# Native float32 transforms in place of split ones, and four weight tiles converted at other places

## The chip, the cores and the metric

The kernel runs on one core of a Trainium2 chip. The time is that of one execution on the device, in microseconds (us). The engines work side by side, each through its own list of instructions in order: TensorE (PE) multiplies matrices, VectorE (DVE) and ScalarE (ACT) work elementwise, GpSimd (POOL) does elementwise work and issues DMAs, SyncE (SP) issues DMAs.

## The reference

Three layers follow one another. Attention has 4 batches, 8 heads, 512 local and 32 global tokens and a head width of 64; the middle layer is a gated feed-forward with a convolution of width 3 over the tokens; the last mixes tokens and features by a Fourier transform, then has a layernorm and an MLP.

```python
# x: attention output, [4, 544, 512]
h = np.maximum(x @ w_in, 0.0)                       # w_in [512, 1024]
conv_out[:, s] = sum(conv_w[k] * h[:, s + k - 1] for k in range(3))
x = (h / (1.0 + np.exp(-conv_out))) @ w_out         # w_out [1024, 512]
mixed = np.real(np.fft.fft(np.fft.fft(x, axis=1), axis=2))
u = x + mixed
un = (u - mean(u)) / np.sqrt(var(u) + 1e-06)
out = u + np.maximum(un @ w_ch1, 0.0) @ w_ch2       # 512 -> 2048 -> 512
```

All weights come as float64. A tile of weights is made from their raw 32-bit halves on the chip.

## The kernel before, in words

**Splitting.** The products of the middle layer and the MLP keep both factors as two rounded parts (`fp32r`), high and low, and `mm3` (L145) issues three matmuls for each product: low by high, high by low, high by high. In attention the matmuls take plain float32 (`mm` alone), as the scores of `s_mm` (L284): two row blocks and two heads, 224 columns each, a head on 64 of the 128 rows. L339 and L340 are float32 transposes.

**Weight tiles.** The MLP has 32 of them, 0 to 15 of `ch1` and 16 to 31 of `ch2`, each 512 KB raw. To make one, `fetch` has SP load the raw tile; `from_f64` takes ACT L164, POOL L165, ACT L167 and DVE L171 and L172; `put` writes the high part by ACT (L200) and the low part by DVE (L201). Tiles KEEP1 to 31 are converted during the attention steps (`keep_load`, `keep_make`, `keep_store`; the first of them at step KEEP0, then one each two steps) and put into device memory (`kept`). Later POOL loads them from there (`fetch_c`, L731). The others are fetched and converted (`make_c`) from the last MoE units on, and in the first NCONV = 5 steps of the MLP.

**The stages.** Attention and most of the MoE run interleaved, in an order written out by hand. Then comes the MoE tail: the loop over units u (64 units, 16 for each batch; each has `m_g1` into one PSUM bank `g1`, relu h at L482, the convolution on ACT and DVE at L492 to L494, tanh at L500, the gate g at L511 to L513, and `m_g2`). With it run four blocks a unit of the first transform. The MLP has 128 steps v, 16 for each chunk c of 272 tokens: `c_g1` (banks `g1` and `pv` in turn), relu and split into `hdt` (L798, L799), `c_g2` into the banks a0 to a3 with a tile `w_v`. The three other transforms run in its first five steps. From the MoE tail on, a scheduler orders the instructions by priority and by the places in SBUF that they need.

**The transform.** `fft(b)` is a generator of 13 pieces for one batch. It folds the tokens (L653, L656, L657 on DVE), splits the folded tile `ff` into `fh` and `fl` (ACT L654, L658; DVE L655, L659), multiplies with the constants c2, s2 and the single row co (six blocks of 256 or 258 columns), takes each block from PSUM as a high part by ACT (L672, L679) and a low part by DVE (L673, L680) into `ab`, and multiplies these with c1 and s1 (five blocks of 274 columns, DVE evacuates: L693, L696, L703, L706, L714, L715). The blocks go to the banks `s` and `t` in turn. In the trace c2 and c1 are both called `c`, s2 and s1 both `s`. Constants are split as well, so a block takes nine matmuls for three products.

**Places.** Some places in SBUF have names, v16 to v31; raw tiles, weight tiles and the tiles of the transform take them one after another. A tile that takes a place waits until all readers of the one before are done.

## Time and profile before

| | |
|---|---|
| median of three runs | 836.88 us (836.75, 836.88, 844.13) |
| profiled execution | 841.99 us, span 840.2 us |
| mean granted clock of PE | 0.968 |
| PE busy | 789.2 us (94% of the span) |
| DVE busy | 463.1 us (55%) |
| ACT busy | 372.2 us (44%) |
| POOL busy | 213.5 us (25%) |

The profiled execution is one of its own, so its time stands beside the median of the others. The clock is a share of full speed, 2.4 GHz: 1.00 is the upper level, 0.50 the lower (1.2 GHz). A busy share is a mean over stages that differ, so the sections below go by stretches. A matmul's own duration is that of one in flight; several overlap, and their price is the time from start to start.

### The profile page before, as it was taken

The numbers are of one execution on the slowest core, as the hardware profiler recorded it, in microseconds if no ns is written. First come the engines' busy times: TensorE is split into PE (matmuls) and PEld (weight loads), VectorE is DVE, ScalarE is ACT, GpSimd is POOL, SyncE is SP. The second block draws the span as 40 slices with busy tenths as digits, with TensorE's granted clock in tenths as the row PEclk, the third lists the DMA queues.
The fourth block names the chain that finished last, engine by engine and source line by source line (L and its number), as shares of the span: only waits on it lengthen the run. The fifth ranks groups of instructions, "written<-read, shape, count | busy, mean of one in ns | idle before, by whom it ended". The sixth has DMA issues, their size and how long they took to land.

```text
span 840.2 us, 16148 instructions
## 1 busy us (share of the span) xinstructions
PE 789.2 (94%) x6436; PEld 741.4 (88%) x6436; DVE 463.1 (55%) x1202; ACT 372.2 (44%) x947; POOL 213.5 (25%) x274
## 2 busy tenths in 40 slices
PE   5769999999999989987798999999999999999997
PEld 3458889899889879986697999999999999999997
DVE  5898987778777785699797531222222122222212
ACT  5677776666666765666652132121211212121110
POOL 4554443222222230122241252040402204030100
PEclk9789999999999998998988999999999999999999
DMA  7743341354136420664301700000000000000000
GB/s 248 265 151 112 127 160 57 113 176 156 40 109 207 145 76 2 176 183 125 126 1 50 253 27 1 2 27 1 28 1 28 2 1 27 1 28 1 27 2 27
DMA packets 32299, 69.06 MB, mean 82 GB/s; under 512 B 2728, under 2 KB 19496, under 8 KB 32224
## 3 DMA queue, kind: packets, MB, share of 16 engines
q1 hardware_dynamic: 29664, 59.08, 20.8%
q0 software_dynamic: 2560, 8.94, 3.6%
q8 instruction: 51, 0.84, 0.4%
q14 instruction: 24, 0.20, 0.1%
HBM read 57.65 MB, written 10.75 MB: 81 GB/s over the span
## 4 chain that ended last, share of the span: by engine, by line
PE 62%; DVE 14%; DMA 11%; ACT 9%; issue 2%; POOL 1%; SPq 0%; DVEq 0%; ACTq 0%; POOLq 0%
PE ps_a L143 28%; PE ps_g L143 16%; PE ps_pv L143 11%; DMA raw_r<-in_ch_dram 6%; PE ps_s L143 4%; ACT pb L318 3%; PE ps_t L143 2%; DVE y L493 2%; DVE pb L306 2%; DMA raw_w<-in_ch_dram 1%; DVE y L494 1%; DVE mag L172 1%; DMA co<-in_co_dram 1%; ACT mag L164 1%; DVE mag L171 1%
## 5 line engine op out<-in xcount | busy, mean ns | idle before, releaser
L143 PE MATMUL ps_a<-hdt,w_v 128*128 128x272 f32 x1536 | 215.3, 289 | 0.2 <-DVE w_v L201 0.2
L143 PEld LDWEIGHTS ps_a<-hdt,w_v 128*128 128x128 f32 x1536 | 202.2, 190 | 0.5 <-DVE w_v L201 0.5
L143 PE MATMUL ps_g<-xh,w_w 128*128 128x256 f32 (+1 forms) x512 | 116.0, 305 | 3.6 <-ACT h L482 3.5
L143 PE MATMUL ps_a<-g,w_w 128*128 128x254 f32 (+1 forms) x768 | 113.4, 296 | 5.0 <-ACT g L512 4.9
L329 POOL TENSOR_SCALAR pb<-pb,sm 128x224 f32<-128x224 f32 x128 | 83.2, 666 | 134.9 <-DVE sm L324 105.7
L143 PE MATMUL ps_g<-chl,w_w 128*128 128x272 f32 x768 | 108.1, 288 | 0.9 <-DVE chl L763 0.9
L143 PEld LDWEIGHTS ps_a<-g,w_w 128*128 128x128 f32 x768 | 103.4, 193 | 6.3 <-ACT g L512 5.4
L143 PE MATMUL ps_pv<-chl,w_w 128*128 128x272 f32 x768 | 107.0, 288 | 0.0
L143 PEld LDWEIGHTS ps_g<-chl,w_w 128*128 128x128 f32 x768 | 100.7, 188 | 1.3 <-DVE chl L763 1.1
L143 PEld LDWEIGHTS ps_pv<-chl,w_w 128*128 128x128 f32 x768 | 100.5, 188 | 0.0
L143 PEld LDWEIGHTS ps_g<-xh,w_w 128*128 128x128 f32 x512 | 87.2, 194 | 13.6 <-issue 7.9
L799 DVE SCALAR_TENSOR_TENSOR hdt<-ps_pv,hdt 128x272 fp32r<-128x272 f32 x64 | 28.2, 440 | 125.5 <-ACT hdt L798 125.5
L799 DVE SCALAR_TENSOR_TENSOR hdt<-ps_g,hdt 128x272 fp32r<-128x272 f32 x64 | 28.0, 438 | 113.3 <-ACT hdt L798 113.3
L798 ACT ACTIVATE hdt<-ps_pv 128x272 fp32r<-128x272 f32 x64 | 25.3, 396 | 139.5 <-PE ps_pv L143 134.2
L798 ACT ACTIVATE hdt<-ps_g 128x272 fp32r<-128x272 f32 x64 | 25.4, 397 | 135.6 <-PE ps_g L143 130.1
L143 PE MATMUL ps_g<-xl,w_w 128*128 128x256 f32 (+1 forms) x256 | 75.6, 295 | 0.0
L820 POOL TENSOR_TENSOR misc<-misc,u 128x272 f32<-128x272 f32 x28 | 19.3, 719 | 213.0 <-DVE misc L819 213.0
L318 ACT ACTIVATE pb<-pb,sm 128x224 f32<-128x224 f32 x128 | 60.4, 475 | 12.8 <-DVE sm L306 12.7
L165 POOL TENSOR_SCALAR mag<-mag 128x512 f32<-128x512 f32 x36 | 28.8, 801 | 93.3 <-ACT mag L164 92.7
L143 PE MATMUL ps_s<-qk 64*128 64x224 f32 (+1 forms) x144 | 38.0, 427 | 13.8 <-DMA qk<-in_qk_dram 6.7
L143 PEld LDWEIGHTS ps_g<-xl,w_w 128*128 128x128 f32 x256 | 49.8, 195 | 0.0
L493 DVE SCALAR_TENSOR_TENSOR y<-h,convw,y 128x254 f32<-128x254 f32 (+1 forms) x64 | 35.2, 550 | 16.2 <-ACT y L492 16.0
(206 smaller groups left out, 1269.4 us busy)
## 6 DMA issues: line engine op xcount, KB each, us to landing
v<-in_v_dram SPq DMA_DIRECT2D x16, 640.0 KB, 4.6
raw_w<-in_ch_dram SPq DMA_DIRECT2D x16, 512.0 KB, 3.7
qk<-in_qk_dram SPq DMA_DIRECT2D x16, 464.0 KB, 6.0
raw_r<-in_ch_dram SPq DMA_DIRECT2D x12, 512.0 KB, 6.3
kept<-w_o SPq DMA_DIRECT2D x12, 512.0 KB, 5.3
w_v<-kept POOLq DMA_DIRECT2D x12, 512.0 KB, 4.7
qk<-in_qk_dram SPq DMA_DIRECT2D x16, 304.0 KB, 6.0
out_dram<-misc SPq DMA_DIRECT2D x32, 136.0 KB, 1.7
```

Source lines behind the costliest of these rows:

```text
L143: return pe.matmul(o, a, b, start=start, stop=stop)
L164: act.activation(mag, f32(head), AF.Abs, scale=65536.0)
L165: (clamp or dve).tensor_scalar(mag, mag, TOP, 2.0, op0=ALU.min, op1=ALU.max)
L171: dve.scalar_tensor_tensor(val, val, 3, tail, op0=ALU.logical_shift_left, op1=ALU.bitwise_or)
L172: dve.scalar_tensor_tensor(val, head, -(2**31), val, op0=ALU.bitwise_and, op1=ALU.bitwise_or)
L306: anchor[i] = dve.tensor_tensor_reduce(out=pbs(i)[h][:, a, 0:224], in0=sb[h][:, a], in1=mask[:, 2 * where(i)[1] + a], scale=-0.125, scalar ...
L318: act.activation(p, p, AF.Exp, bias=sm[:, k:k + 1], scale=-1.0, accum_out=sm[:, 4 + k:5 + k])
L329: gp.tensor_scalar(p, p, sm[:, k:k + 1], 1.0, op0=ALU.mult, op1=ALU.mult)
L493: dve.scalar_tensor_tensor(y, hb[:, cc - 1:cc - 1 + n], convw2[:, m, 0:1], y, op0=ALU.mult, op1=ALU.add)
L798: act.activation(hd[:, 0], o, AF.Relu)
L799: dve.scalar_tensor_tensor(hd[:, 1], o, 0.0, f32(hd[:, 0]), op0=ALU.max, op1=ALU.subtract)
L820: (dve if c == 7 else gp).tensor_add(o, o, u_t[b][:, e, HS * half:HS * half + HS])
```

## The change

The transforms take float32 as it is. The splits of the folded tile and of the blocks are gone (`ff`, `fh`, `fl` become one tile `fi` written by DVE; `ab` holds one copy made by ACT), the constants are not split and half as large, and each product is one native matmul. The constants are loaded by SP and no longer by POOL. Tile 19 is one more that is converted in attention (KEEP0, KEEP1 = 8, 19). Tiles 16 to 18 are fetched at the start of the MoE tail into places v29 to v31, which the transform no longer needs, and converted in units 56 to 58, ahead of tiles 0 to 7. In the first MLP steps tiles 8 to 15 alone are converted. The places of the transform's tiles are dealt anew: c2 and s2 share v20, c1 has v21, s1 v24, `fi` v22 and v23 in turn, `ab` v25 and v27 in turn.

```diff
--- before.py
+++ after.py
@@ -31,7 +31,7 @@
 SOLO = 8
 LAG_G2 = 3
 NCONV = 5
-KEEP0, KEEP1 = 10, 20
+KEEP0, KEEP1 = 8, 19
 NPB, NHB = 3, 3
 MT = [(0, 92), (92, 92), (184, 90)]
 
@@ -52,17 +52,6 @@
     t2 = (DM - p) % DM
     t2[0] = DM // 2
     return np.concatenate([p, 128 + p, t2, DM // 2 + 128 - p])
-
-
-def _round12(x):
-    m, e = np.frexp(np.asarray(x, np.float64))
-    return np.ldexp(np.round(m * 4096.0) / 4096.0, e)
-
-
-def _split(x):
-    hi = _round12(x)
-    lo = _round12(x - hi)
-    return np.stack([hi, lo], axis=-2).astype(np.float32)
 
 
 def _constants():
@@ -105,10 +94,10 @@
     s1[:, 272] = 0.0
 
     def tok(x):
-        return _split(x.reshape(3, 92, NF).transpose(1, 0, 2))
+        return x.reshape(3, 92, NF).transpose(1, 0, 2).astype(np.float32)
 
     def feat(x):
-        return _split(x.reshape(2, 128, -1).transpose(1, 0, 2))
+        return x.reshape(2, 128, -1).transpose(1, 0, 2).astype(np.float32)
 
     return {
         "ident": np.eye(128, dtype=np.float32),
@@ -630,12 +619,13 @@
     frp = right.enter_context(tc.tile_pool(name="frp", bufs=1, side="right"))
     u0 = frp.tile([128, 4, 546], F32, name="u0")
     fp = right.enter_context(tc.tile_pool(name="fp", bufs=1, side="right"))
-    c2 = fp.tile([128, 2, 2, 258], F32R, tag="v20", name="c2")
-    s2 = fp.tile([128, 2, 2, 256], F32R, tag="v21", name="s2")
-    co = fp.tile([1, 258], F32R, name="co")
-    c1 = fp.tile([128, 2048], F32R, tag="v25", name="c1")
-    s1 = fp.tile([128, 2048], F32R, tag="v27", name="s1")
-    c1, s1 = [t[0:92, 0:6 * NF].rearrange("p (t s k) -> p t s k", t=3, s=2) for t in (c1, s1)]
+    c2s2 = fp.tile([128, 1028], F32, tag="v20", name="c2s2")
+    c2 = c2s2[:, 0:516].rearrange("p (c k) -> p c k", c=2)
+    s2 = c2s2[:, 516:1028].rearrange("p (c k) -> p c k", c=2)
+    co = fp.tile([1, 258], F32, name="co")
+    c1 = fp.tile([128, 1024], F32, tag="v21", name="c1")
+    s1 = fp.tile([128, 1024], F32, tag="v24", name="s1")
+    c1, s1 = [t[0:92, 0:3 * NF].rearrange("p (t k) -> p t k", t=3) for t in (c1, s1)]
     u_t = {}
 
     turn = itertools.cycle("st")
@@ -645,39 +635,29 @@
 
     def fft(b):
         eo = eo_t[b]
-        ff = fp.tile([128, 1024], F32, tag="v24", name="ff")
-        fe = fd = ff[:, 0:2 * NF].rearrange("p (c n) -> p c n", c=2)
-        fh = fp.tile([128, 4, NF], F32R, tag="v22", name="fh")
-        fl = fp.tile([128, 4, NF], F32R, tag="v23", name="fl")
+        fi = fp.tile([128, 4, NF], F32, tag=f"v{22 + b % 2}", name="fi")
         rev = slice(S, S - NF, -1)
-        dve.tensor_add(fe, eo[:, 0:2, 0:NF], eo[:, 0:2, rev])
-        act.copy(fh[:, 0:2], fe)
-        dve.tensor_sub(fl[:, 0:2], fe, f32(fh[:, 0:2]))
-        dve.tensor_sub(fd, eo[:, 2:4, 0:NF], eo[:, 2:4, rev])
-        dve.tensor_add(fd[0:1, 0], eo[0:1, 2, 0:NF], eo[0:1, 2, rev])
-        act.copy(fh[:, 2:4], fd)
-        dve.tensor_sub(fl[:, 2:4], fd, f32(fh[:, 2:4]))
+        dve.tensor_add(fi[:, 0:2], eo[:, 0:2, 0:NF], eo[:, 0:2, rev])
+        dve.tensor_sub(fi[:, 2:4], eo[:, 2:4, 0:NF], eo[:, 2:4, rev])
+        dve.tensor_add(fi[0:1, 2], eo[0:1, 2, 0:NF], eo[0:1, 2, rev])
         yield
-        ab = fp.tile([128, 3084], F32R, tag="v29", name="ab")
-        ah, al = [ab[0:92, 774 * i:774 * i + 774].rearrange("p (t k) -> p t k", t=3) for i in range(2)]
-        bh, bl = [ab[0:92, 1548 + 768 * i:2316 + 768 * i].rearrange("p (t k) -> p t k", t=3) for i in range(2)]
+        ab = fp.tile([128, 2048], F32, tag=f"v{25 + 2 * (b % 2)}", name="ab")
+        at = ab[0:92, 0:774].rearrange("p (t k) -> p t k", t=3)
+        bt = ab[0:92, 774:1542].rearrange("p (t k) -> p t k", t=3)
         for t, (n0, nn) in enumerate(MT):
             ns = slice(n0, n0 + nn)
             o = fbank()[0:nn, 0:258]
             for c in range(2):
-                mm3(o, fh[:, c, ns], fl[:, c, ns], c2[:, c, 0], c2[:, c, 1], c == 0, False)
-            mm(o, fl[0:1, 2, ns], co, False, False)
-            mm(o, fh[0:1, 2, ns], co, False, True)
+                mm(o, fi[:, c, ns], c2[:, c], c == 0, False)
+            mm(o, fi[0:1, 2, ns], co, False, True)
             with pri("fev"):
-                act.copy(ah[0:nn, t], o)
-                dve.tensor_sub(al[0:nn, t], o, f32(ah[0:nn, t]))
+                act.copy(at[0:nn, t], o)
             yield
             o = fbank()[0:nn, 0:256]
             for c in range(2):
-                mm3(o, fh[:, 2 + c, ns], fl[:, 2 + c, ns], s2[:, c, 0], s2[:, c, 1], c == 0, c == 1)
+                mm(o, fi[:, 2 + c, ns], s2[:, c], c == 0, c == 1)
             with pri("fev"):
-                act.copy(bh[0:nn, t], o)
-                dve.tensor_sub(bl[0:nn, t], o, f32(bh[0:nn, t]))
+                act.copy(bt[0:nn, t], o)
             yield
         if b not in u_t:
             u_t[b] = up.tile([128, 4, 546], F32, tag="u", name="u") if b else u0
@@ -687,7 +667,7 @@
             fs = slice(128 * c, 128 * c + 128)
             o = fbank()[:, 0:NF]
             for t, (n0, nn) in enumerate(MT):
-                mm3(o, ah[0:nn, t, fs], al[0:nn, t, fs], c1[0:nn, t, 0], c1[0:nn, t, 1], t == 0, t == 2)
+                mm(o, at[0:nn, t, fs], c1[0:nn, t], t == 0, t == 2)
             e = eo[:, c]
             with pri("fev"):
                 dve.scalar_tensor_tensor(
@@ -697,7 +677,7 @@
             yield
             o = fbank()[:, 0:NF]
             for t, (n0, nn) in enumerate(MT):
-                mm3(o, bh[0:nn, t, fs], bl[0:nn, t, fs], s1[0:nn, t, 0], s1[0:nn, t, 1], t == 0, t == 2)
+                mm(o, bt[0:nn, t, fs], s1[0:nn, t], t == 0, t == 2)
             q = eo[:, 2 + c]
             with pri("fev"):
                 dve.scalar_tensor_tensor(
@@ -709,7 +689,7 @@
             yield
         o = fbank()[0:1, 0:NF]
         for t, (n0, nn) in enumerate(MT):
-            mm3(o, ah[0:nn, t, 256:257], al[0:nn, t, 256:257], c1[0:nn, t, 0], c1[0:nn, t, 1], t == 0, t == 2)
+            mm(o, at[0:nn, t, 256:257], c1[0:nn, t], t == 0, t == 2)
         r = ut[0:1, 2]
         dve.tensor_add(r[:, 0:HS + 1], r[:, 0:HS + 1], o[:, 0:HS + 1])
         dve.tensor_add(r[:, back], r[:, back], o[:, 1:HS])
@@ -718,7 +698,9 @@
     ch1, ch2 = {}, {}
 
     def c_slot(i):
-        return (wp, f"w{i}") if i < 16 else (lw if i < 20 else fp, f"v{i}")
+        if 16 <= i < 19:
+            return fp, f"v{i + 13}"
+        return (wp, f"w{i}") if i < 16 else (lw if i == 19 or i > 28 else fp, f"v{i}")
 
     @prio("cv")
     def fetch_c(i, n=1):
@@ -821,7 +803,7 @@
                 sp.dma_start(out[128 * e:128 * e + 128, HS * c:HS * c + HS], o)
 
     for t, nm in ((c2, "c2"), (s2, "s2"), (c1, "c1"), (s1, "s1"), (co, "co")):
-        gp.dma_start(t, d[nm])
+        sp.dma_start(t, d[nm])
     ffts = [fft(b) for b in range(4)]
     fq = ffts[0:1]
 
@@ -834,6 +816,9 @@
             except StopIteration:
                 queue.pop(0)
 
+    for i in range(16, 19):
+        fetch_c(i)
+    early = [16, 17, 18]
     lnq = []
     ln0 = 0
     for u in range(ulast + 1, NM + LAG_G2):
@@ -859,6 +844,8 @@
             fetch_c(8 + k - 3)
         if 0 <= k - 3 < 8:
             make_c(k - 3)
+        elif early and k >= 0:
+            make_c(early.pop(0))
     while ln0 < 6:
         step(lnq)
         ln0 += 1
@@ -866,14 +853,14 @@
     lw = ctx.enter_context(tc.tile_pool(name="lw", bufs=1))
     misc = xp.tile([128, 8, HS], F32, tag="xl", name="misc")
     mags += [misc[:, 2 * i:2 * i + 2].rearrange("p a c -> p (a c)")[:, 0:512] for i in (3, 1, 2)]
-    for i in range(16, 20):
+    for i in (19, 29, 30, 31):
         fetch_c(i)
     while lnq:
         step(lnq)
     f3 = ffts[1:]
     nstep = 13 * len(f3)
     done = 0
-    order = [x for v in range(4) for x in (16 + v, 8 + v)] + [12, 13, 14, 15]
+    order = list(range(8, 16))
     for v in range(128 + 2):
         c, m = divmod(v, 16)
         if v < NCONV:
@@ -886,7 +873,7 @@
             for x in order[len(order) * v // NCONV:len(order) * (v + 1) // NCONV]:
                 make_c(x)
             if v == NCONV - 1:
-                for i, n in ((25, 2), (27, 2), (29, 3)):
+                for i, n in ((25, 2), (27, 2)):
                     fetch_c(i, n)
                 dead[1] = frp.tile([128, 4, 546], F32, tag="u", name="u")
         if m == (NCONV if c == 0 else 4) and c + 1 < 8:
```

On PE, at the end of the last transform's blocks, before: the names `w_v` are MLP weight tiles, `ps_a` the four banks of `c_g2`.

```order
L143 MATMUL ps_t<-c_4344,fh 90x258 x2
L143 MATMUL ps_t<-co,fl 90x258
L143 MATMUL ps_t<-co,fh 90x258
L143 MATMUL ps_s<-s_4345,fl 90x256
L143 MATMUL ps_s<-s_4345,fh 90x256 x2
L143 MATMUL ps_s<-s_4345,fl 90x256
L143 MATMUL ps_s<-s_4345,fh 90x256 x2
L143 MATMUL ps_t<-c_4347,ab 128x274 x9
L143 MATMUL ps_s<-s_4348,ab 128x274 x9
L143 MATMUL ps_a_5371<-hdt,w_v_5528 128x272 x3
```

The same place after; `w_v_5291` is the tile in place v20, which follows c2 and s2 (`c2s`) there.

```order
L132 MATMUL ps_t<-c2s_4357,fi 90x258 x2
L132 MATMUL ps_t<-co,fi 90x258
L132 MATMUL ps_s<-c2s_4357,fi 92x256 x2
L132 MATMUL ps_t<-c_4359,ab 128x274 x3
L132 MATMUL ps_s<-c2s_4357,fi 90x256 x2
L132 MATMUL ps_t<-c_4359,ab 128x274 x3
L132 MATMUL ps_s<-s_4360,ab 128x274 x3
L132 MATMUL ps_t<-c_4359,ab 1x274 x3
L132 MATMUL ps_a_5185<-hdt,w_v_5291 128x272 x3
L132 MATMUL ps_a_5186<-hdt,w_v_5291 128x272 x3
```

A first-stage block has two or three matmuls in place of eight or six, a second-stage block three in place of nine, and the last first-stage blocks stand close ahead of the products with w_v_5291.

On ACT, at the passage from attention's last steps to the MoE tail, before: L482 is the relu h, L492 the convolution, L500 the tanh and L512 the gate.

```order
L512 CAST g<-y 128x254
L654 CAST fh<-ff 128x548
L482 ACTIVATE h_93<-ps_g_4297 128x256
L492 ACTIVATE y<-h_93,convw_61 128x254
L658 CAST fh<-ff 128x548
L500 ACTIVATE y<-y 128x254
L482 ACTIVATE h_94<-ps_g_4355 128x256
L492 ACTIVATE y<-h_94,convw_61 128x254
L512 CAST g<-y 128x254
L500 ACTIVATE y<-y 128x254
```

After, where the same lines are L471, L481, L489 and L501, and L153 and L156 belong to `from_f64`:

```order
L435 CAST xh<-ps_s 128x2x32
L501 CAST g<-y 128x254
L471 ACTIVATE h_93<-ps_g_4310 128x256
L481 ACTIVATE y<-h_93,convw_61 128x254
L153 ACTIVATE mag<-raw_v_4366 128x512
L156 ACTIVATE raw_v_4366<-raw_v_4366 128x512
L153 ACTIVATE mag<-raw_v_4368 128x512
L156 ACTIVATE raw_v_4368<-raw_v_4368 128x512
L489 ACTIVATE y<-y 128x254
L471 ACTIVATE h_94<-ps_g_4373 128x256
L156 ACTIVATE raw_v_4370<-raw_v_4370 128x512
L481 ACTIVATE y<-h_94,convw_61 128x254
```

The two splits of the transform's folded tile are gone; the conversions of tiles 16 to 18 (`raw_v_4366`, `raw_v_4368`, `raw_v_4370`) stand ahead of a tanh and an h.

On SP, the raw loads of the tail before:

```order
L179 DMA raw_w_4507<-in_ch_dram 128x4x256
L179 DMA raw_w_4596<-in_ch_dram 128x4x256
L179 DMA raw_w_4641<-in_ch_dram 128x4x256
L179 DMA raw_w_4689<-in_ch_dram 128x4x256
L179 DMA raw_w_4687<-in_ch_dram 128x4x256
```

And after, with three raw tiles and the constants (L806) ahead of them:

```order
L168 DMA raw_v_4366<-in_ch_dram 128x1024
L168 DMA raw_v_4368<-in_ch_dram 128x1024
L168 DMA raw_v_4370<-in_ch_dram 128x1024
L806 DMA c2s_4357<-in_c_dram 128x516
L806 DMA c2s_4357<-in_s_dram 128x512
L806 DMA c_4359<-in_c_dram 92x822
L806 DMA s_4360<-in_s_dram 92x822
L806 DMA co<-in_co_dram 1x258
L168 DMA raw_w_4480<-in_ch_dram 128x4x256
L168 DMA raw_w_4554<-in_ch_dram 128x4x256
```

The constants are new in this queue, and stand behind three raw tiles.

## Rows read from the trace of the kernel before

**Rows 1.** Busy time by stage: stretch, length; busy (instructions) of PE, PEld, DVE, ACT, POOL; clock.

```profile
75.00:110.00 35.00, 33.00 (x315) 29.79 (x315) 33.24 (x91) 25.88 (x73) 15.47 (x19) 1.00 0.27 90
370.00:400.00 30.00, 21.32 (x124) 18.85 (x124) 26.83 (x50) 19.88 (x40) 7.86 (x5) 0.83 0.42 126
400.00:425.00 25.00, 21.07 (x137) 19.21 (x136) 19.52 (x39) 14.79 (x28) 8.56 (x6) 0.87 0.29 107
425.00:462.00 37.00, 33.73 (x222) 29.18 (x221) 31.02 (x62) 14.18 (x30) 8.77 (x11) 0.90 0.09 27
462.00:498.50 36.50, 36.50 (x293) 36.12 (x292) 15.94 (x32) 8.02 (x17) 13.31 (x16) 1.00 0.44 147
498.50:832.00 333.50, 333.50 (x2668) 333.50 (x2667) 79.16 (x160) 62.75 (x139) 57.51 (x56) 1.00 0.04 13
338.70:498.50 159.80, 143.86 (x1006) 133.55 (x1005) 117.94 (x232) 78.53 (x163) 41.87 (x40) 0.93 0.37 116
```

**Rows 2.** The same view in stretches of 5 us.

```profile
420.00:425.00 5.00, 5.00 (x24) 5.00 (x23) 5.00 (x10) 2.92 (x5) 3.87 (x2) 0.50 0.01 3
455.00:460.00 5.00, 5.00 (x22) 3.85 (x21) 0.85 (x2) 1.03 (x3) 0.53 (x1) 0.54 0.00 0
```

**Rows 3.** Waits of PE from 338.7 to 498.5 us: total, times, longest.

```profile
PE ps_a L143 <- ACT g L512: 4.9, 2, 4.5
PE ps_g L143 <- ACT h L482: 2.2, 1, 2.2
PE ps_s L143 <- DVE u L706: 1.9, 1, 1.9
```

**Rows 4.** Waits of ACT from 338.7 to 462 us.

```profile
ACT raw_w L167 <- DMA raw_w<-in_ch_dram: 10.3, 9, 2.4
```

**Rows 5.** Timeline of ACT at 373 us: start, duration, instruction, idle time ahead.

```profile
373.61 0.67 ACT L167 ACTIVATE raw_w<-raw_w 128x512 int32<-128x512 uint32 x1 [1.61 <-DMA raw_w<-in_ch_dram]
374.17 0.39 ACT L482 ACTIVATE h<-ps_g 128x292 f32<-128x292 f32 x1
```

**Rows 6.** Timeline of PE at 368 us.

```profile
368.42 0.29 PE L143 MATMUL ps_g<-xh,w_w 128*128 128x292 f32 x1
368.56 1.30 PE L143 MATMUL ps_s<-c,ab 92*128 92x274 f32 x9
369.70 0.30 PE L143 MATMUL ps_g<-xh,w_w 128*128 128x292 f32 x1
```

**Rows 7.** Timeline of PE in attention, at 200.8 and 204.3 us.

```profile
200.84 0.35 PE L143 MATMUL ps_s<-qk 64*128 64x224 f32 x1
200.84 0.35 PE L143 MATMUL ps_t<-qk 64*128 64x224 f32 x1
201.03 0.35 PE L143 MATMUL ps_s<-qk 64*128 64x224 f32 x1
...
204.35 0.27 PE L340 MATMUL ps_s<-ident,pb 128*128 128x128 f32 x1
204.46 0.27 PE L339 MATMUL ps_s<-ident,pb 128*128 128x128 f32 x1
```

**Rows 8.** Groups by line and form, 338.7 to 498.5 us: count, busy us, mean ns.

```profile
L172 DVE SCALAR_TENSOR_TENSOR mag<-raw_w,mag 128x512 int32<-128x512 int32 x8 | 5.4, 678 | 0.0
...
L659 DVE TENSOR_TENSOR fl<-ff,fh 128x548 fp32r<-128x548 f32 x4 | 2.9, 715 | 0.3 <-ACT fh L658 0.3
...
L658 ACT CAST fh<-ff 128x548 fp32r<-128x548 f32 x4 | 2.6, 646 | 2.4 <-DVE ff L657 2.4
...
L673 DVE TENSOR_TENSOR ab<-ps_t,ab 92x258 fp32r<-92x258 f32 x4 | 1.7, 414 | 1.8 <-ACT ab L672 1.8
```

**Rows 9.** DMA issues, 330 to 500 us: count, KB each, median us from issue to landing.

```profile
raw_w<-in_ch_dram SPq DMA_DIRECT2D x16, 512.0 KB, 3.7
w_v<-kept POOLq DMA_DIRECT2D x12, 512.0 KB, 4.7
...
s<-in_s_dram POOLq DMA_DIRECT2D x1, 590.8 KB, 8.9
```

## The prediction

> **What bounds the kernel now.** I read the busy time by stage first. From 498.50 us to 832 us TensorE (PE) holds 333.50 of 333.50 us in 2,668 matmuls, 0.125 us each [rows 1]: the MLP after its first chunk is PE at its rate, and the change doesn't touch it. In attention, 75 to 110 us, DVE is busy 33.24 of 35.00 us and PE 33.00 [rows 1]; both are close to full. What lies between is the place of the change: 338.70 to 498.50 us, where PE is busy 143.86 of 159.80 us at a granted clock of 0.93 [rows 1]. Within it 370 to 400 us has PE at 21.32 of 30.00 us (clock 0.83), 400 to 425 us at 21.07 of 25.00 us (0.87), and 425 to 462 us at 33.73 of 37.00 us (0.90); from 462 us it is full again [rows 1]. So PE loses time twice over: it stands still, and after each longer stand (or thin stretch of DFT) it runs at the lower level, 1.2 GHz: 0.50 in 420 to 425 us, 0.54 in 455 to 460 us [rows 2].
>
> Then the waits of PE in that stretch, to see who makes it stand: gate tiles from ACT (4.9 us, of which one is 4.5), the relu h from ACT (one of 2.2), and many small ones on DVE's stage-2 evacuation of the DFT (1.9 is the largest group) [rows 3]. Behind the two ACT waits is something else: ACT itself waited 10.3 us, nine times, for raw weight tiles to land [rows 4]. The moment shows it: at 373.61 us ACT starts the L167 of a tile for which it waited 1.61 us, and the h that PE needs comes right behind it at 374.17 us [rows 5]. ACT executes in order, so a conversion put ahead of its data blocks the MoE tail.
>
> **How much PE work there is before and after.** Before, the stretch holds 656 matmuls of MoE and MLP and 348 of the DFT (1,006 by the window's count, which cuts two at its edges [rows 1]). Of the 656, 416 have 272 columns at 0.125 us, 192 have 290 or 292 columns at 0.13 us (368.42 to 368.56 [rows 6], rounded down for 290), and 48 have 254 or 256, about 0.118: 52.0 + 25.9 + 5.7 = 83.6 us. The DFT's nine matmuls of 274 columns take 1.14 us (368.56 to 369.70 [rows 6]), 0.127 each; one transform has 45 such, and 42 of 256 or 258 columns at about 0.12 (estimated from the 274 by columns): 5.7 + 5.0, and with some 0.4 for the six that have a single input row, 11.2 us, four times 44.8. Together 128.4 us of work in 159.8: 31.4 us are lost, some 16 by standing (159.80 less 143.86), the rest by the lower clock and by drains that the trace counts as busy.
>
> After, a transform has 30 native float32 matmuls in place of 87. Their price stands in attention, where the scores are native: four matmuls of 224 columns for two heads, on 64 rows each, show as two instances a matmul, and the heads' instances start in pairs, 0.19 us from pair to pair (200.84, 201.03 [rows 7]), 0.85 ns a column. A pair may be two halves of the array at work together, and then a full-height instance costs the same 0.19; or one after the other, and then half. The row nearest to a full-height instance is a float32 transpose of 128 columns, a single instance: 204.35 to 204.46, 0.11 us, 0.85 ns a column [rows 7]. So I take two instances of 0.85, 1.70 ns a column, against 0.46 for one product now; the half of it is a rival below. By columns: 15 of 274 at 0.465, 9 of 258 at 0.438, 6 of 256 at 0.434, 7.0 + 3.9 + 2.6 = 13.5 us, four times 54.1. **PE gets 9.3 us more work**, not less. A run with no stall at all would then need 83.6 + 54.1 = 137.7 us, 22.1 below the 159.8 of now. The net of the tail is 22.1 less the stalls S that remain or are new.
>
> The Trainium skill ("FP8 and Floating Point Precision", TensorE Precision Notes) says that true FP32 makes four passes through the array. Four passes at the 0.46 ns of a product would be 1.85 ns a column, 14.8 us a transform and 59.1 us for four, 5 us more than by the rows; the forecast below would then be 835.6. The trace has 1.70, so I stay with that.
>
> **What is taken from DVE and ACT.** Gone are the splits: per transform L655 and L659 (715 ns each [rows 8]) and six of L673 and L680 (414 ns) on DVE, 8 x 0.715 + 24 x 0.414 = 15.7 us for four; and on ACT one L654 and one L658 (646 ns [rows 8]), 5.2 us. DVE's 117.94 busy us in the stretch [rows 1] become about 100 with one conversion fewer (three operations like L172's 0.68 [rows 8]). It was never full over the stretch, but from 370 to 400 us it had 26.83 of 30.00 [rows 1], and there it counts.
>
> **What is moved.** (a) Tile 19 is converted in attention, at step 8, the twelve others keep their steps. That is 2.0 us of DVE, and about as much of ACT, where DVE has 1.76 us free in 35 [rows 1]; so between 0 and 2 us, I take 0.9. (b) Tiles 16 to 18 are loaded and converted at steps 56 to 58, in the row of ACT ahead of tanh and h. Their three loads stand in SP's queue just before the constants, which came by POOL's queue so far and took 8.9 us for the last large one [rows 9]. At the front the first raw tile has no cover: the usual load takes 3.7 us from issue [rows 9], and ACT stands at its L153 with tanh and h behind. That is 0.5 to 2, I take 1.5. The constants are half as large, but come behind 1.57 MB; now 2.2 MB take 8.9 us, so the 1.57 and the 0.26 of c2 take about 7.4, and c2 is there some 342 us after the start. By the order the first DFT block comes behind the first products of unit 56, a little later: no wait, by about 1 us. (c) In the MoE tail and the first MLP steps the tiles 0 to 15 stay where they are; four fewer conversions stand among the first MLP steps (eight in place of twelve), which is where 400 to 425 us is thin. The long native DFTs make a unit of MoE tail longer (5 to 6 us), so loads of 3.7 us land in time, and the 4.5 and 2.2 us waits shrink.
>
> **The walk.** I went along the new order of PE with these durations, and held against it when DVE, ACT and the loads can deliver. What stays: 1.5 at the front (b); about 5.3 where the MoE ends and the first layernorm feeds the MLP (two gates, the first chl and the bank t: 1.3, 2.1, 1.4, 0.5, still bound by DVE and by order); 1.2 at the banks pv and g1; 0.8 in the stretch with only DFT (27 matmuls of 274 columns and 30 of 256 or 258, 12.6 + 13.1 = 25.7 us of PE, about as long as DVE needs for the evacuations beside it); 1.2 for the 12 changes to a one-row matmul; **1.7 at w_v20**, a new wait: its place is that of c2 and s2, which the last first-stage block frees only some 4 us of PE before its own first matmul, while a kept tile takes 4.7 us to land [rows 9] and POOL must issue it; and 3.2 (2.5 to 4) at the lower clock, in place of some 10 now. Sum S = 14.9, between 10 and 22. The tail gains 22.1 less 14.9, 7.2 us; less 0.9 in attention, **6.3 us**. The profiled execution took 841.99 us for a span of 840.2, 5.1 over the median; I put the difference on the median: 836.88 - 6.3 = 830.6, some 0.8%. No change is told from one of under 1% by a measurement of this kernel.
>
> **Rivals.** *The stalls go.* If ACT no longer waits for raw tiles and DVE keeps ahead with 18 us less, S falls to 4 or 5: the gain is 17 and the time 820. For it: 10.3 us of ACT's waits [rows 4] are the cause of the two longest stands of PE and of the low clock behind them [rows 2], and long native matmuls give everyone time. Against it: the end of the MoE hangs on a chain through DVE that the change leaves.
>
> *The gain is eaten.* The stalls only move: S is 22, as much as there is to gain, and the time is 838. For it: PE gets 9.3 us more work for certain, the gain is all in waits, and a wait removed shows the next one.
>
> *Slower: a DFT stretch at the lower clock.* Now 452 to 460 us, with DFT alone, runs at 0.54 [rows 2], although PE is busy in it. After, 25.7 us of PE work stand as blocks of DFT alone over two banks in turn, each waiting for its copy by ACT or its two DVE operations. If all of it ran at 1.2 GHz it would take 25.7 us longer: 830.6 + 25.7 = 856. It ends slower than before by 1% once about 15 us of the stretch are at the lower level (6.3 + 8.4). Against it: matmuls of 0.45 us leave PE busy without gaps, where the short ones now drained between blocks, and attention holds 1.00 over 75 to 110 us with native matmuls in it [rows 1].
>
> The Trainium skill ("TensorE: Matmul & The Clock Gate", A second HAM failure mode: psum-queue depth-cycling) describes a clock that swings between its levels when matmul groups cycle through PSUM banks and PE idles a little between them. The 0.54 above is in line with it; by that rule the rival would hold for the whole stretch.
>
> *Native costs half.* If the pairs of rows 7 run one after the other, the DFT takes 27 us and PE 17.8 less than now; with 21 us of stalls, since DVE and the loads then come late more often, the stretch is 132 and the time 836.88 - 28 + 0.9 = 810. Against it stands the transpose.
>
> **How the numbers follow.** Chances: the forecast 0.40 (825 to 836), stalls go 0.26 (815 to 825), gain eaten 0.18 (836 to 844), lower clock 0.10 (846 to 856), native at half 0.06 (about 810). The range of 8 in 10 leaves out the last two and the edge of the second: 816 to 844. Faster by over 1% is below 828.5: 0.26 + 0.06 + a quarter of the forecast, 0.42. Slower by over 1% is above 845.2: 0.10 and a trace of the third, 0.12. Within 1%: 0.46.
>
> **What would show it.** In the profile after: 120 native matmuls as 240 instances, at some 0.23 us from start to start; PE busy more than 143.86 us between the first g1 of unit 55 and the end of chunk 0, in a shorter stretch; no L655, L659, L673 or L680 on DVE; ACT's waits for raw tiles well below 10.3 us but one at 339 us ahead of tanh; a wait of PE for w_v20 on the DMA; the clock at 0.5 for under 7 us. Attention should end at most 2 us later. The prediction is wrong if the native price is not 1.70 ns a column, if DFT blocks run at the lower clock, or if PE waits longer for ACT at steps 56 to 58 than for one landing.

## The result, and the profile after

The changed kernel takes 848.40 us (median of 16 runs, 843.17 to 852.24), the kernel before 840.24 us in runs beside it (832.05 to 846.25). The ratio is 1.0103 with a 95% interval of 1.0075 to 1.0130: slower by 1%, outside the predicted range and with the other sign. The profiled execution took 844.94 us for a span of 843.2, only 3.0 above that of before. Two executions of one kernel differ by several us in where the clock falls: in the six traces here whose attention is that of the kernel before, unit 8 begins anywhere from 93.7 to 96.1 us. So the places are read from traces and the sizes from the ratios.

The busy time by stage of the changed kernel comes first (columns as in [rows 1]; two more stand at the end, the share and the GB/s of the DMA engines). The last row is the stretch from the first g1 matmul of MoE unit 55 to the end of chunk 0 (DVE's first evacuation of its banks), which before is 338.73 to 497.57 us. I call it the tail.

```profile
75.00:110.00 35.00, 31.94 (x306) 28.88 (x307) 32.35 (x89) 26.25 (x73) 15.47 (x19) 1.00 0.27 91
370.00:400.00 30.00, 24.29 (x121) 19.04 (x120) 27.55 (x52) 21.53 (x43) 10.62 (x7) 0.80 0.53 164
400.00:425.00 25.00, 25.00 (x156) 22.34 (x155) 20.80 (x38) 13.93 (x28) 7.18 (x9) 0.89 0.31 106
425.00:462.00 37.00, 34.81 (x159) 22.37 (x158) 13.88 (x29) 5.20 (x14) 1.63 (x3) 1.00 0.13 43
498.50:832.00 333.50, 333.50 (x2666) 333.50 (x2665) 79.57 (x161) 62.65 (x139) 57.83 (x56) 1.00 0.04 13
...
340.52:500.73 160.21, 151.38 (x896) 124.65 (x895) 103.25 (x196) 71.53 (x153) 37.01 (x39) 0.95 0.33 106
```

The same view of before for its own tail, and behind it, for both kernels, MoE units 8 to 14 in attention (from the first g1 matmul of unit 8 to that of unit 14; before, then after).

```profile
338.73:497.57 158.84, 142.90 (x999) 132.59 (x998) 117.01 (x230) 78.48 (x163) 41.45 (x39) 0.92 0.37 116
...
96.14:125.84 29.70, 29.61 (x248) 26.75 (x248) 27.08 (x77) 23.27 (x65) 12.77 (x17) 1.00 0.41 132
```

```profile
93.80:130.23 36.43, 31.35 (x251) 27.90 (x249) 29.22 (x82) 24.86 (x67) 13.55 (x19) 0.95 0.42 146
```

Three things are to be seen. In units 8 to 14 the same PE work takes 36.43 us in place of 29.70: PE, which was full there, stands for 5 us and loses clock. The tail takes 160.21 us in place of 158.84, although PE stands less in it (8.83 us against 15.94). A difference as small as this isn't sharp, since other traces with the same code for the tail show 162.15 for that of before and 160.03 to 160.72 for the changed one (table below). And DVE's load in the tail has fallen by 13.8 us, as the splits are gone, without an earlier end.

What PE waits for in units 8 to 14, in the timeline of the changed kernel:

```profile
99.09 0.42 PE L132 MATMUL ps_s<-qk 64*128 64x224 f32 x1 [2.09 <-DMA qk<-in_qk_dram]
...
121.24 0.43 PE L132 MATMUL ps_s<-qk 64*128 64x224 f32 x1 [2.29 <-DMA qk<-in_qk_dram]
```

Before has no wait of PE for qk in these units. SP's queue tells why. First before, then after:

```profile
85.53 0.33 SPq L276 DMA_DIRECT2D v<-in_v_dram  x1
85.91 0.77 SPq L179 DMA_DIRECT2D raw_r<-in_ch_dram  x1
86.73 0.90 SPq L269 DMA_DIRECT2D qk<-in_qk_dram  x2
101.47 0.33 SPq L276 DMA_DIRECT2D v<-in_v_dram  x1
```

```profile
84.74 0.33 SPq L265 DMA_DIRECT2D v<-in_v_dram  x1
92.40 0.33 SPq L250 DMA_DIRECT2D kept<-w_o  x1
92.78 0.42 SPq L168 DMA_DIRECT2D raw_r<-in_ch_dram  x1
93.26 1.33 SPq L258 DMA_DIRECT2D qk<-in_qk_dram  x2
101.19 0.33 SPq L265 DMA_DIRECT2D v<-in_v_dram  x1
114.33 0.33 SPq L250 DMA_DIRECT2D kept<-w_o  x1
114.71 1.71 SPq L168 DMA_DIRECT2D raw_r<-in_ch_dram  x1
116.47 0.91 SPq L258 DMA_DIRECT2D qk<-in_qk_dram  x2
```

The store of tile 19 (`kept<-w_o`, L250) is a new instruction of SP. It waits until DVE has made the tile, and DVE is busy 7.54 of the 7.70 us from 84.70 to 92.40. SP stands there from 85 to 92.40 us, and the two qk loads behind it go out at 93.26 us, where before they went out at 86.73. The next store, of tile 20, is held up again, from 101.5 to 114.33 us; before, it went out at 108.01. The waits of SP in 84 to 130 us name the same (before, then after):

```profile
SPq L261 <- DVE w_o L201: 6.1, 1, 6.1
```

```profile
SPq L250 <- DVE w_o L190: 23.9, 3, 12.8
```

### The profile page after: what moved, and what is told of

Read it like the earlier page. It is cut to its first block, busy times and chain, and to the rows that moved or that the text cites. A ratio compares the mean times of both kernels' runs of the same rounds, so it can differ in the third digit from the quotient of the medians.

```text
span 843.2 us, 15916 instructions
## 1 busy us (share of the span) xinstructions
PE 797.4 (95%) x6328; PEld 733.0 (87%) x6328; DVE 449.7 (53%) x1170; ACT 366.4 (43%) x939; POOL 205.3 (24%) x270
## 4 chain that ended last, share of the span: by engine, by line
PE 64%; DVE 15%; DMA 10%; ACT 8%; issue 1%; SPq 1%; POOL 0%; DVEq 0%; ACTq 0%; POOLq 0%
PE ps_a L132 27%; PE ps_g L132 16%; PE ps_pv L132 12%; DMA raw_r<-in_ch_dram 6%; PE ps_s L132 4%; PE ps_t L132 4%; DVE pb L295 2%; ACT pb L307 2%; DMA raw_w<-in_w_in_dram 2%; DVE y L482 2%; DVE y L483 2%; DVE mag L161 1%; ACT mag L153 1%; DMA qk<-in_qk_dram 1%; DVE mag L160 1%
## 5 line engine op out<-in xcount | busy, mean ns | idle before, releaser
L154 POOL TENSOR_SCALAR mag<-mag 128x512 f32<-128x512 f32 x40 | 32.7, 817 | 84.0 <-ACT mag L153 81.8
L482 DVE SCALAR_TENSOR_TENSOR y<-h,convw,y 128x254 f32<-128x254 f32 (+1 forms) x64 | 35.6, 556 | 13.5 <-ACT y L481 13.3
```

The lines of the kernel that those rows point to most:

```text
L154: (clamp or dve).tensor_scalar(mag, mag, TOP, 2.0, op0=ALU.min, op1=ALU.max)
L482: dve.scalar_tensor_tensor(y, hb[:, cc - 1:cc - 1 + n], convw2[:, m, 0:1], y, op0=ALU.mult, op1=ALU.add)
```

## The experiments

Ratios are to the kernel before, in runs beside it on the same chip; 0.1% is 0.84 us. "Units 8 to 14" and "tail" are lengths in one profiled execution. A tail has a spread of some us: e1_dft_only, g4_dft_again and f3_dft_late have the same code for it, and show 155.13, 154.99 and 158.87. In the diffs, "..." stands for lines not shown. The scheduler makes its order anew from the MoE tail on, so an edit there can change the order of other instructions too.

| kernel | ratio (95%) | units 8 to 14 | tail |
|---|---|---|---|
| changed kernel | 1.0103 (1.0075 to 1.0130) | 36.43 | 160.21 |
| e1_dft_only | 0.9909 (0.9877 to 0.9942) | 29.79 | 155.13 |
| e2_no19 | 0.9959 (0.9936 to 0.9981) | 30.09 | 157.29 |
| e3_att19 | 1.0101 (1.0055 to 1.0146) | 38.68 | 158.37 |
| e4_noearly | 1.0209 (1.0168 to 1.0249) | 36.37 | 172.45 |
| f1_after_late | 1.0011 (0.9981 to 1.0041) | 30.69 | 160.03 |
| f2_before_late | 0.9978 (0.9947 to 1.0009) | 29.70 | 162.15 |
| f3_dft_late | 0.9955 (0.9923 to 0.9987) | 30.89 | 158.87 |
| f4_no19_gp | 0.9982 (0.9950 to 1.0013) | 30.26 | 160.86 |
| g1_dft_att19_late | 1.0064 (1.0035 to 1.0093) | 30.42 | 160.53 |
| g2_dft_sp | 1.0129 (1.0097 to 1.0162) | 30.32 | 171.81 |
| g3_late_gp | 0.9968 (0.9941 to 0.9996) | 30.50 | 158.06 |
| g4_dft_again | 0.9943 (0.9913 to 0.9974) | 29.96 | 154.99 |
| h1_att19_late | 1.0015 (0.9986 to 1.0045) | 30.42 | 158.77 |
| h2_after_again | 1.0081 (1.0052 to 1.0110) | 38.11 | 160.72 |
| h3_late_again | 1.0042 (1.0017 to 1.0067) | 30.71 | 160.52 |

**The change in its parts.** Four kernels of one chip: the transforms alone, the change without tile 19, tile 19 alone, and the change without the early conversions.

```diff
 e1_dft_only (from the changed kernel)
-KEEP0, KEEP1 = 8, 19
+KEEP0, KEEP1 = 10, 20
...
-        sp.dma_start(t, d[nm])
+        gp.dma_start(t, d[nm])
...
-    for i in range(16, 19):
-        fetch_c(i)
-    early = [16, 17, 18]
...
-    for i in (19, 29, 30, 31):
+    for i in range(16, 20):
         fetch_c(i)
...
-    order = list(range(8, 16))
+    order = [x for v in range(4) for x in (16 + v, 8 + v)] + [12, 13, 14, 15]
...
```

Not shown are the places of tiles 16 to 18, the call that converts them early, and the loads of tiles 29 to 31, all as in the kernel before.

> Native float32 transforms alone; all weight tiles are converted where the kernel before does it, the constants come by POOL. Theory A (the tail: 9 to 12 us more PE work in the transforms and the stalls that stay at the end of the MoE eat the whole saving): slower than before by 4 to 8 us, most of the changed kernel's 8. Theory B (the conversion of tile 19 in attention and its load ahead of qk): within 2 us of before, or up to 4 faster. Theory C (tiles 16 to 18 at units 56 to 58): within 2 us of before.

Measured: 0.9909, 6.5 us faster by the medians (834.07 against 840.60). Theory A falls: the transforms alone gain, and more than theories B and C had.

```diff
 e2_no19 (from the changed kernel)
-KEEP0, KEEP1 = 8, 19
+KEEP0, KEEP1 = 10, 20
...
-    order = list(range(8, 16))
+    order = [19] + list(range(8, 16))
```

> The changed kernel, but tile 19 is converted in the first MLP steps and not in attention. Theory A: no change from the changed kernel, about 1% above before. Theory B: 4 to 6 us below the changed kernel, so within 4 us of before, and in the profile attention ends about 1.8 us earlier. Theory C: as A.

Measured: 0.9959. Without tile 19 in attention the change is faster than before, by 2.9 us of the medians, and units 8 to 14 take 30.09 us. The changed kernel on this chip (h2_after_again, in a later session) is 10.7 us slower, about twice what theory B had.

```diff
 e3_att19 (from the kernel before)
-KEEP0, KEEP1 = 10, 20
+KEEP0, KEEP1 = 8, 19
...
-    order = [x for v in range(4) for x in (16 + v, 8 + v)] + [12, 13, 14, 15]
+    order = [x for v in range(3) for x in (16 + v, 8 + v)] + [11, 12, 13, 14, 15]
```

> The kernel before, with tile 19 alone moved from the first MLP steps to attention. Theory A: within 1.5 us of before (the first MLP steps get one conversion fewer). Theory B: 4 to 6 us slower than before. Theory C: as A.

Measured: 1.0101, 9.2 us by the medians, more than theory B asked for. The old transforms with tile 19 alone in attention are as slow as the whole change. Units 8 to 14 take 38.68 us, 9.0 more than before.

```diff
 e4_noearly (from the changed kernel)
...
-    for i in range(16, 19):
-        fetch_c(i)
-    early = [16, 17, 18]
...
-    order = list(range(8, 16))
+    order = [x for v in range(3) for x in (16 + v, 8 + v)] + [11, 12, 13, 14, 15]
...
```

> The changed kernel, but tiles 16 to 18 are fetched and converted in the first MLP steps as before, not at units 56 to 58. Theory A: the time of the changed kernel, 1% above before, within 2 us. Theory B: the same. Theory C (ACT stands behind three early raw loads, and the loads of tiles 0 to 15 come later): 4 to 8 us below the changed kernel.

Measured: 1.0209, against all three theories. Its units 8 to 14 are those of the changed kernel, but the tail has 12 us more. That was a new question, taken up with g2_dft_sp.

**Where tile 19 costs.** Theory H: the store holds the qk loads in SP's queue. The test changes only the place of the stores.

```diff
 f1_after_late (from the changed kernel); f2, f3, g1, g3, h1 and h3 have the same edit
+        pend = None
...
             if live and i > 0:
                 load_qk(i + 1)
+            keep_store(pend)
...
-            keep_store(keep_tile(i, 1))
+            pend = keep_tile(i, 1)
+            if i > NU:
+                keep_store(pend)
```

> The changed kernel with the store of each kept tile issued by SP behind the next qk load and not ahead of it; nothing else is moved. Theory H (SP stands at the store of tile 19, which waits for DVE, and the qk loads stand behind it): the 8 to 11 us of tile 19 go for the most part, the time is 3 to 9 us below the changed kernel's, so between 7 below before and 3 above it. Rival W (the work of the conversion itself in a full DVE, and the traffic of its load): no change, 1% above before.

Measured: 1.0011, within theory H's range; the changed kernel's 1.0103 came from another session. SP's queue now reads:

```profile
86.02 0.33 SPq L265 DMA_DIRECT2D v<-in_v_dram  x1
86.39 0.43 SPq L168 DMA_DIRECT2D raw_r<-in_ch_dram  x1
86.87 0.42 SPq L258 DMA_DIRECT2D qk<-in_qk_dram  x1
93.65 0.33 SPq L250 DMA_DIRECT2D kept<-w_o  x1
94.08 0.38 SPq L258 DMA_DIRECT2D qk<-in_qk_dram  x1
```

The first qk load goes out at 86.87 us, as before the change, and the store still waits until 93.65. Units 8 to 14 by the view of busy time, PE nearly full again:

```profile
95.05:125.74 30.69, 29.71 (x251) 26.63 (x249) 29.29 (x83) 23.36 (x66) 12.95 (x17) 1.00 0.44 151
```

So the conversion's work stayed (DVE 29.29 us) and the 6 us of units 8 to 14 went: there, it is the queue.

> The kernel before with tile 19 in attention, as e3_att19, but with the stores behind the qk loads. Theory H: within 3 us of before, where e3_att19 was 1.0% above it; units 8 to 14 take about 30.5 us in the profile, not 38.7. Rival W: 5 to 9 us above before.

This is e3_att19 with the edit above. Measured: 1.0015, where e3_att19 had 1.0101. Units 8 to 14 take 30.42 us, where they took 38.68. Theory H holds with the old transforms too: by the medians 6.7 of the 9.2 us go.

> The changed kernel itself on the chip of the two others: about 1% above before, units 8 to 14 at about 36 us.

> The changed kernel with the stores behind the qk loads, beside the changed kernel on one chip. Theory H: 5 to 9 us below h2_after_again. Rival W: within 2 us of it.

Measured beside each other on one chip: 848.39 and 845.10 us, 1.0081 and 1.0042. The changed kernel's excess halves; 3.3 us are less than the 5 to 9 that I expected, though units 8 to 14 shrink by 7.4 us (38.11 to 30.71). Of these, 1.5 us come back between units 14 and 50 (189.94 and 191.44 us in the two traces; the seven kernels with late stores show 189.8 to 193.3 there, the ten others 188.4 to 189.9). With the two chips of f1_after_late and h3_late_again, the place of the store is worth 0.4 to 0.9%. It isn't all that tile 19 costs: h3_late_again is still 7.4 us slower than e2_no19 (837.71 us, the same chip in an earlier session), which has no tile 19 in attention. No run here shows where these lie; in single traces 3.2 us of them are in the tail.

> The kernel before with the same move of the stores. Theory H: the trace of before has the same wait of SP, shorter (the first store at 102 to 108 us), without a wait of PE for qk there, so 0 to 3 us faster. Rival W: no change.

Measured: 0.9978, not to be told from no change. SP's shorter waits in the kernel before cost nothing that can be told.

> Native transforms alone (as in e1_dft_only) with the same move of the stores. Theory H: 0 to 3 us below e1_dft_only, so 6 to 10 below before, and the fastest version so far. Rival W: as e1_dft_only, 6.5 below before.

Measured: 0.9955, 3.8 us below before and no better than the transforms without it (0.9909 and 0.9943, on other chips). Theory H had 6 to 10 below before, rival W 6.5; neither is met. No gain shows where tile 19 isn't in attention.

**The constants.** They came by POOL's queue and now come by SP's.

```diff
 f4_no19_gp (from e2_no19), g3_late_gp (from f1_after_late)
-        sp.dma_start(t, d[nm])
+        gp.dma_start(t, d[nm])
```

> The changed kernel without tile 19 in attention (as e2_no19), with the constants loaded by POOL as before. If the place of the constants in SP's queue behind three raw tiles is what e2_no19 loses against e1_dft_only (3.6 us): 2 to 4 us below e2_no19, about 0.9% below before. If it is the early conversion of tiles 16 to 18 itself, or the order that follows from it: as e2_no19, 0.4% below before.

Measured: 0.9982, not lower than e2_no19's 0.9959. With tiles 16 to 18 early and tile 19 out of attention, the queue of the constants makes no difference that can be told.

> The changed kernel with the stores behind the qk loads and the constants by POOL. Theory Q: 2 to 5 us below f1_after_late, so 0.2 to 0.5% below before. Theory C (what is left comes from the early conversions): as f1_after_late, level with before.

Measured: 0.9968, where f1_after_late had 1.0011 and its repetition 1.0042: 0.4 to 0.7% lower, with a tail of 158.06 us. This fits theory Q, but the chips differ, and f4_no19_gp speaks the other way.

```diff
 g2_dft_sp (from e1_dft_only)
-        gp.dma_start(t, d[nm])
+        sp.dma_start(t, d[nm])
```

> Native transforms alone, with the constants loaded by SP in place of POOL. Theory Q (in SP's queue the constants come late or delay the raw tiles, which made e4_noearly 18 us slower): 5 to 12 us above native alone. If e4_noearly was slow by the meeting of tile 19 and the order that followed, and not by the queue: within 2 us of native alone.

Measured: 1.0129, beside 0.9943 for the same kernel with POOL: 16 us for this one line, more than theory Q's range. It isn't the queue alone, since the scheduler's order changes with it: PE's first product with c2 starts at 341.78 us in g4_dft_again and earlier, at 337.47, here (unit 55 starts at 336.0 in both). The tail grows from 154.99 to 171.81 us, by the same 17 us by which e4_noearly's stands above e1_dft_only's; e4_noearly has the same wait for `co` (4.2 us), so I take this for its cause too. PE's timeline shows the first link, a wait for the one-row constant `co`:

```profile
342.11 0.30 PE L132 MATMUL ps_g<-xh,w_w 128*128 128x292 f32 x1
346.63 1.16 PE L132 MATMUL ps_s<-co,fi 1*92 1x258 f32 x2 [4.23 <-DMA co<-in_co_dram]
```

The rest of the 17 us is not one wait; the second raw load goes out at 355.04 us where it was 345.45, and the clock falls three times more. In this kernel POOL issues three loads of kept tiles in the same 2 us as SP the constants; in g4_dft_again POOL issues both, one after the other, and has no such wait. Whether these make `co` late wasn't tried.

> Native transforms, tile 19 in attention with the stores behind the qk loads, constants by POOL; tiles 16 to 18 are converted in the first MLP steps. Theory H (tile 19 cost what it did by the place of its store): within 3 us of native alone, 0.5 to 0.9% below before. If tile 19 costs by its work too, 4 to 6 us above native alone. Beside g3_late_gp it shows what the early conversion of tiles 16 to 18 does: theory C has this kernel 3 to 5 us below that one.

This is e4_noearly with the late stores and the constants by POOL. Measured: 1.0064, a miss: 10 us above g4_dft_again. Units 8 to 14 are short (30.42), so it isn't theory H's cost; the tail is 5.5 us longer. PE waits there for a kept tile; these are rows of PE's and of POOL's timeline:

```profile
457.51 1.55 PE L132 MATMUL ps_t<-c,ab 92*1 92x274 f32 x6
...
466.74 3.29 PE L132 MATMUL ps_a<-hdt,w_v 128*128 128x272 f32 x14 [6.00 <-DMA w_v<-kept]
```

```profile
396.10 0.59 POOL L715 DMA_DIRECT2D w_v<-kept  x1 [11.36 <-DVE hdt L756]
...
459.57 1.59 POOL L715 DMA_DIRECT2D w_v<-kept  x3 [1.16 <-issue]
```

It isn't tile 19 that comes late: POOL loads it at 396.10 us, and PE uses it some 22 us later. The wait is ahead of the sixth group of `c_g2`, that of tile 21, whose place is that of c1. The last block with c1 starts at 457.51, the load is one of the three behind it, and PE, after one more product of `c_g1`, stands until it has landed. In g4_dft_again the same group starts without a wait. So this passage has another order with tile 19 in attention, and that is where the wait comes from. The two traces differ by 5.8 us of span; the rest of the 10 us doesn't show in them, since the execution that was profiled is the fastest of g1_dft_att19_late (840.72, median 845.72).

> Native transforms alone once more, on the chip of the three others, so that they can be held against it: 0.6 to 1.2% below before.

Measured: 0.9943, beside 0.9909 on the first chip. The native transforms alone beat both kernels, and no other version here beats them.

## Why the prediction was wrong

**The step that failed is (a), tile 19 in attention: "between 0 and 2 us, I take 0.9".** It costs 9.2 us with the old transforms (e3_att19; 9.0 of them in units 8 to 14) and 10.7 in the changed kernel (h2_after_again against e2_no19). Of the 14.5 us between the forecast, 6.3 faster, and the result, 8.2 slower, it makes up 9.8; the other 4.7 lie in the tail and are taken up below. I priced the conversion as work of DVE and ACT, and looked at the raw load. But a tile has three entries in attention: the load, the conversion, and the store. The store is SP's, stands ahead of two qk loads, and waits for the end of a conversion that is slow because DVE is full (7.54 of 7.70 us). The premise "DVE has 1.76 us free in 35" was right; its consequence is that the tile is finished late (92.40 us), and everything behind it in a queue in order pays the delay, not the work. That "the twelve others keep their steps" is true of the program and not of the time: the next store was held for 12.8 us. f1_after_late and h1_att19_late show the mechanism, since they move the store by one entry and units 8 to 14 return to 30.4 to 30.7 us. It explains 6.7 of 9.2 us with the old transforms; in the changed kernel, on one chip, 3.3 of 10.7, and the cause of the rest stays open.

**The price of a native matmul was right per block, low in sum.** Three matmuls of 274 columns follow one another in 1.39 us, 0.464 each (forecast 0.465). These are the rows of the changed kernel's timeline:

```profile
443.78 1.10 PE L132 MATMUL ps_t<-c2s,fi 128*90 128x256 f32 x4
444.72 1.03 PE L132 MATMUL ps_s<-c2s,fi 128*90 128x258 f32 x4
445.68 0.67 PE L132 MATMUL ps_s<-co,fi 1*90 1x258 f32 x2
446.28 1.66 PE L132 MATMUL ps_t<-s,ab 92*128 92x274 f32 x6
447.77 1.55 PE L132 MATMUL ps_s<-c,ab 92*128 92x274 f32 x6
449.16 1.55 PE L132 MATMUL ps_t<-s,ab 92*128 92x274 f32 x6
```

That is 1.69 ns a column, and the rival "native costs half" is out. But two matmuls of 258 columns take 0.96 us, not 0.88 (1.86 ns a column), two of 256 take 0.94, and the one-row matmul 0.60, not 0.44. By these rows a transform is 14.5 us and four are 57.8, where I had 54.1 and 1.2 for changes to one-row matmuls. The Trainium skill ("FP8 and Floating Point Precision", TensorE Precision Notes) has true FP32 make four passes, from which the prediction estimated 1.85 ns a column and 59.1 us. The trace has less in the blocks of 274 columns and as much in those of 258, so that estimate came nearer to the sum.

**The tail.** At the lower level a matmul takes twice as long: two of 258 columns took 1.96 us (394.77 to 396.73), as these rows of the changed kernel show, behind a stand of PE for the gate.

```profile
389.68 3.27 PE L132 MATMUL ps_a<-g,w_w 128*128 128x290 f32 x12 [2.87 <-ACT g L501]
...
394.77 2.03 PE L132 MATMUL ps_t<-c2s,fi 128*92 128x258 f32 x4 [1.38 <-DVE u L743]
396.73 1.17 PE L132 MATMUL ps_t<-co,fi 1*92 1x258 f32 x2
```

So half of PE's busy time at 0.50 is lost to the clock. These are all such stretches of the tail, before, then after, then with the transforms alone (e1_dft_only).

```profile
374.25:377.66 3.41, 3.04 (x12) 2.97 (x13) 2.12 (x5) 2.56 (x7) 0.56 (x1) 0.50 0.18 62
384.49:391.31 6.82, 4.40 (x18) 4.27 (x19) 6.60 (x11) 5.64 (x13) 2.33 (x3) 0.50 0.18 63
418.62:425.45 6.83, 6.18 (x27) 6.21 (x28) 6.83 (x15) 3.11 (x5) 4.60 (x3) 0.50 0.01 2
452.76:459.58 6.82, 6.59 (x27) 5.10 (x25) 2.90 (x7) 1.11 (x4) 0.27 (x1) 0.50 0.03 10
```

```profile
388.30:405.30 17.00, 14.24 (x44) 10.34 (x45) 15.01 (x24) 11.32 (x21) 4.80 (x5) 0.50 0.19 59
```

```profile
383.71:390.53 6.82, 5.50 (x19) 4.47 (x20) 5.37 (x9) 4.77 (x10) 0.83 (x2) 0.50 0.08 12
...
335.67:490.80 155.13, 146.63 (x896) 122.10 (x895) 105.24 (x199) 73.62 (x156) 34.77 (x39) 0.98 0.35 112
```

That is 10.1 us lost before, 7.1 after and 2.8 with the transforms alone. What is left of PE's busy time is its work at full clock: 132.8, 144.3 and 143.9 us. So the changed kernel's tail has 11.5 more work, 7.1 less standing and 3.0 less clock: 1.4 us longer, and not 7.2 shorter. The forecast of the added work, 9.3 and 1.2, was nearly right. With the transforms alone the same sum is 11.1, 7.4 and 7.4: 3.7 shorter.

**The stalls.** S was to be 14.9 above 137.7 us of work. On that scale the trace has 22.5 (160.21 less 137.7). Standing is 8.8 of it, where my terms made 10.5: the front came to 0.8 us (forecast 1.5), the end of the MoE to 5.5 (4.1 for the gate, 1.4 for L743; forecast 5.3), w_v20 to 0.5, as a wait of the weight load (forecast 1.7). Below are the longest waits of PE in the tail, and that one.

```profile
PE ps_a L132 <- ACT g L501: 4.1, 2, 2.9
PE ps_t L132 <- DVE u L743: 1.4, 1, 1.4
PE ps_s L132 <- DVE u L686: 1.0, 1, 1.0
PE ps_g L132 <- ACT h L471: 0.8, 1, 0.8
...
PEld ps_a L132 <- DMA w_v<-kept: 0.5, 1, 0.5
```

Two other terms were mis-sized. The clock took 7.1, where I had 3.2; it is one stretch of 17 us at the end of the MoE, and begins while PE stands the 2.87 us for the gate. And PE was busy 6.6 us beyond the 137.7 at full clock, where I had only the 1.2 for one-row matmuls. The kernel before has such an excess too, some 5 us above my count of its matmuls. The prediction put it there to "drains that the trace counts as busy", and gave it no term after the change, without a reason. What it consists of isn't shown. (In that count, 192 matmuls at the 0.13 us stated are 25.0 us and not 25.9, so its sums are 0.9 too high as they stand.)

So the half of the argument on the transforms had the right sign and, in the tail's trace, half the size (3.7 of 7.2). There the clock took 2.8 us, close to the 3.2, and the excess of busy time is what the forecast lacked. That the transforms alone gain 4.5 to 6.5 in time, about the 6.3 forecast for the whole change, is in part luck. What else is moved in the tail seems to give some of it back. f4_no19_gp against e1_dft_only has tiles 16 to 18 early as the main difference, and is 0.4 to 0.7% slower; since it was on another chip and g1_dft_att19_late shows how much the order matters, the share of the early conversions stays open.

**The rivals.** Slower did come, but not by my slower rival: the stretch that ends in DFT alone, 425 to 462 us, ran at 1.00 (first table). The Trainium skill ("TensorE: Matmul & The Clock Gate", A second HAM failure mode: psum-queue depth-cycling) tells of a bf16 kernel whose clock swings, where matmul groups cycle through PSUM banks with short idles of PE between. The changed kernel's trace doesn't bear it out there, since the two banks are taken in turn, with stands of up to 0.97 us, and the clock holds. But it doesn't hold in every trace: in f4_no19_gp, after stands of 0.57 and 0.97 us in such blocks, it fell for 3.4 us:

```profile
431.99:435.40 3.41, 3.41 (x9) 2.40 (x9) 2.56 (x6) 0.00 (x0) 0.00 (x0) 0.51 0.00 0
```

"The gain is eaten" came nearest in the tail: its S was 22. "No wait" for the constants held in the changed kernel's trace, yet g2_dft_sp shows 16 us for the same edit without the three raw tiles ahead.

## What to carry to other kernels

A step that is moved must be followed through every instruction that it issues, the last one too: an instruction that waits in a queue in order charges its delay, not its work, to all that stands behind it. Where an engine is nearly full, more work on it can cost little by itself (about 1 us in units 8 to 14 here) and much by what is ordered after its end, so put a store behind the loads that the next step waits for. Without such a wait the move gained nothing that could be told (f2_before_late, f3_dft_late). Time a change in its parts: here the native transforms alone gained 0.6 to 0.9%, and a tile moved on the side lost 1.0% by itself.

## What the runs showed of the hardware

- A native float32 matmul of 274 columns over 92 rows takes 0.464 us from start to start in a row of them; followed by a matmul of split products its block of three takes 1.19 us and not 1.39 (367.23 to 368.42 us of the changed kernel). A single-row one of 258 columns takes 0.60 us from its start to the start of the next block, more than one of 128 rows (0.48).
- The stretch of 425 to 462 us, which ends in blocks of native float32 in two banks in turn, runs at a granted clock of 1.00 in the changed kernel; before, with split products, it had 0.90, and 0.54 in 455 to 460 us [rows 1, rows 2]. In f4_no19_gp blocks of native float32 ran at 0.51 for 3.4 us.
- The clock fell within a stand of PE of 2.87 us and stayed at the lower level for 17 us, although PE was busy 14.24 us of them.
